# Rows 0 and 2, and rows 1 and 3, as the pairs of a feed-forward unit, with a new written-out order

## The chip, the cores and the metric

One core of a Trainium2 chip runs the kernel. The metric is the device time of one execution in microseconds. TensorE (PE) does the matrix products, VectorE (DVE) and ScalarE (ACT) work elementwise, GpSimd (POOL) does small things, and SyncE (SP) issues most DMAs. Each engine works through its own queue in order and waits on semaphores.

## The reference, cut to what matters

Two layers alternate, each twice, on a sequence of 2048 rows of 512 columns in bf16. `ssm_k` has a filter of 2048 taps for every column, so the product of spectra is a long causal convolution along the sequence.

```python
def _A_ref(q, k, v, shift_k, ssm_k, ssm_D):
    k_shift = causal filter of k with 4 taps (shift_k)
    kv = k_shift * v
    y = irfft(rfft(kv padded to 4096) * rfft(ssm_k padded to 4096))[:2048]
    y = y + kv * ssm_D
    return q * y

def _B_ref(x, w_gate, w_up, w_down):
    g = _silu(x @ w_gate)
    u = x @ w_up
    return (g * u) @ w_down

x = A_q
x = x + _A_ref(_layernorm(x), A_k, A_v, A_shift_k, A_ssm_k, A_ssm_D)
x = x + _B_ref(_layernorm(x), B_w_gate, B_w_up, B_w_down)
x = x + _A_ref(_layernorm(x), A_k, A_v, A_shift_k, A_ssm_k, A_ssm_D)
x = x + _B_ref(_layernorm(x), B_w_gate, B_w_up, B_w_down)
```

(The first line of `_A_ref` and its transforms are abridged here.) The convolved values of both layers A are the same, since they depend on k, v and the filter alone; only q, the normed x, differs.

## The kernel before, in words

The sequence is cut in four chunks of 512 rows (`NB = 4`). A chunk is held as 128 partitions by four "decimated rows": row r holds the positions 4p + r. The convolution is done by blocks: the spectra of a chunk of kv (X) and of the filter (G) are made with cosine and sine matrices on TensorE (`fwd`, `inv`, L310 through the helper `mm`, L457, L796), multiplied on VectorE (`product`, L641 to L666), and turned back. In the inverse of the first chunk (`inverse_half`, L782) VectorE first makes sums and differences of spectral slots (`m`, L790): the decimated rows 0 and 2 come from the sums alone, the rows 1 and 3 from the differences alone. TensorE then makes four products for each row (L796), and ScalarE copies the rows to Y (`evacuate_y`, L716).

A unit of feed-forward work is (layer, chunk c, half h): two of the four decimated rows, which `rows_of(h)` names. There are sixteen units, in the order (0,0,0), (0,0,1), (1,0,0), (1,0,1), and so on by chunk. For every unit `apply_norm` (L869) makes mean and reciprocal deviation: by ScalarE (`ln_stats_act`, L819: jk L827 and L833, nm, ve L837) or by VectorE (`ln_stats`, bnst L808, ve L811), and then the power -0.5 on GpSimd (rstd, L839 or L813). The first layer norm gives n (L858 on ScalarE, with nmr from L851, or L863 on VectorE). `prologue` (L878) multiplies n by Y, adds it to x (L902, L905, L907 in the first two units, L885 and L886 in the others), norms again to z, and transposes z: by TensorE in the first two units (ptz L919, copied to zT by L922 and L924), by a DMA of SP (L892) in the others. `ffn` (L931) multiplies zT by the gate and up weights (pf, L310), ScalarE evacuates (sg L965, ht L969), VectorE multiplies (L972), and TensorE multiplies by the down weights (pd, L985). ScalarE copies pd to dn (L1021) and VectorE adds it (L1024), or x goes through TensorE (L944).

Beside the units runs the conversion of the next chunk: the filter's transform (H, L418 and the butterflies L539, L545, L556), G (L580), the 4-tap filter on TensorE with its copy ks (L513) and product (L514), X and the products.

What sets the order: every operation is first recorded with engine, cost and dependences (`Plan.add`); then `Plan.order` (L186) sorts the recorded operations by `ORDER`, a list with one number for each of the 1569 operations, written out by hand or by a search ahead of time. `Plan.order` also gives tiles to buffers: rings such as `pf` (4 PSUM banks), `pd` (2) and `pc` (2), each free once its last reader stands in the order. `Plan.issue` (L216) emits the operations in that order, so that every engine's queue follows it, and puts warm-up matmuls (L1253) into expected pauses of TensorE in the first 32 us of the plan.

`EVEN` (L45) chooses the rows of a unit:

```python
    def row(h, o):
        return h + HP * o if EVEN else HP * h + o
```

and, in `inverse_half`, the PSUM ring of each row:

```python
        pss = [new(("pd", "pf", "pd", "pf")[r] if EVEN else ("pd", "pd", "pf", "pf")[r], "ps", [P, D], F32) for r in range(R)]
```

Of the kernel before, what the change touches and what calls it, by code (L numbers as in the profile page):

```python
# [44 lines left out]
EVEN = False  # L45
# [192 lines left out]
def kernel(  # L238
# [38 lines left out]
    def row(h, o):  # L277
        return h + HP * o if EVEN else HP * h + o

# [1007 lines left out]
```

## Time and profile before

| what | value |
|---|---|
| median of 3 runs | 347.1 us (346.98, 347.1, 347.27) |
| profiled execution: span from first to last instruction | 345.6 us |
| mean granted TensorE clock | 0.999 |
| busy: PE, DVE, ACT, POOL | 337.1, 283.0, 253.6, 46.5 us |
| first feed-forward matmul (pf, unit (0,0,0)) | 35.58 us |
| last matmul starts up to | 342.2 us |
| DMA | 22.96 MB, mean 66 GB/s |

The profiled execution is one more execution of the same program; the page gives its span, and no time of it in the metric's terms, so the 1.5 us between its span and the median stand for what lies around the span. Times inside the profile are microseconds from the first instruction. Instructions of one engine overlap a little at their ends (a VectorE instruction of 0.69 us is followed by the next after 0.61), so sums of a queue go by the distance from start to start.

### The profile page before, as it was taken

How to read it: one execution, taken by the hardware profiler on the slowest of the kernel's cores; microseconds unless marked ns; L12 is line 12 of the kernel's file. 1: busy time of each engine (PE TensorE's matmuls, PEld its weight loads, DVE VectorE, ACT ScalarE, POOL GpSimd, SP SyncE). 2: the span in 40 equal slices, each digit the busy share in tenths (PEclk: the TensorE clock that was granted, in tenths of full speed). 3: DMA queues.
4: the chain of work that ended last, by engine and by line, in shares of the span. 5: the costliest groups of instructions: out<-in, count | busy, mean ns of one | idle time of the engine just before them, and what ended most of it. 6: DMA issues, size and time to landing. Idle time of an engine off the chain costs nothing.

```text
span 345.6 us, 6557 instructions
## 1 busy us (share of the span) xinstructions
PE 337.1 (98%) x2580; PEld 248.8 (72%) x2612; DVE 283.0 (82%) x481; ACT 253.6 (73%) x503; POOL 46.5 (13%) x46
## 2 busy tenths in 40 slices
PE   8998999999999999999999999999999999999996
PEld 7655867858687767868587867767685868777784
DVE  7897999999999998999999999989998525526120
ACT  6889999989976657878899794569684645446361
POOL 4051111104110101111110000110401000001000
PEclk9999999999999999999999999999999999999999
DMA  7999204030111715010104102130101020101011
GB/s 282 334 306 336 51 14 63 15 93 1 32 31 29 172 40 144 13 34 2 31 3 122 32 0 62 31 93 1 32 0 34 30 32 0 32 0 21 11 47 46
DMA packets 42089, 22.96 MB, mean 66 GB/s; under 512 B 33861, under 2 KB 39882, under 8 KB 42058
## 3 DMA queue, kind: packets, MB, share of 16 engines
q1 hardware_dynamic: 41904, 22.47, 25.3%
q8 instruction: 20, 0.33, 0.4%
q14 instruction: 11, 0.09, 0.1%
q10 hardware_dynamic: 154, 0.07, 0.1%
HBM read 12.33 MB, written 2.10 MB: 42 GB/s over the span
## 4 chain that ended last, share of the span: by engine, by line
PE 92%; ACT 5%; POOL 2%; issue 1%; DVE 0%; ACTq 0%
PE pf L310 55%; PE pd L985 28%; PE ps L310 5%; POOL rstd L839 2%; PE ps L457 1%; PE wm L1253 1%; ACT H L418 1%; ACT n L858 1%; PE pt L476 1%; ACT Yk L716 1%; ACT ks L513 0%; ACT ht L969 0%; PE pt L365 0%; ACT sg L965 0%; ACT hs L486 0%
## 5 line engine op out<-in xcount | busy, mean ns | idle before, releaser
L310 PE MATMUL pf<-zT,wu_sb 128*128 128x256 bf16 x896 | 110.4, 273 | 0.9 <-ACT zT L924 0.7
L310 PE MATMUL pf<-zT,wg_sb 128*128 128x256 bf16 x896 | 110.6, 273 | 0.1
L985 PE MATMUL pd<-wd_sb,ht 128*128 128x512 bf16 (+1 forms) x442 | 100.6, 372 | 1.1
L310 PEld LDWEIGHTS <-wu_sb 128*128 128x128 bf16 x896 | 87.7, 98 | 16.6 <-issue 0.9
L310 PEld LDWEIGHTS <-wg_sb 128*128 128x128 bf16 x896 | 87.7, 98 | 15.4
L969 ACT CAST ht<-pf 128x512 bf16<-128x512 f32 x112 | 64.8, 589 | 30.7 <-PE pf L310 29.2
L965 ACT ACTIVATE sg<-pf 128x512 bf16<-128x512 f32 x112 | 65.6, 601 | 19.1 <-PE pf L310 17.2
L985 PEld LDWEIGHTS <-ht 128*128 128x128 bf16 x462 | 45.0, 98 | 45.2 <-DVE ht L972 0.9
L813 POOL TENSOR_TENSOR rstd<-ve,nhalf 128x2 f32<-128x2 f32 x24 | 27.7, 1153 | 204.5 <-DVE ve L811 204.5
L972 DVE TENSOR_TENSOR ht<-ht,sg 128x1024 bf16<-128x1024 bf16 (+1 forms) x64 | 39.0, 620 | 15.2 <-ACT ht L969 10.2
L1021 ACT CAST dn<-pd 128x512 bf16<-128x512 f32 x28 | 16.1, 590 | 24.1 <-PE pd L985 22.9
L808 DVE BATCH_NORM_STATS2 bnst<-xc 128x6 f32<-128x512 bf16 x48 | 31.7, 686 | 0.7
L1024 DVE TENSOR_TENSOR xc<-xc,dn 128x1024 bf16<-128x1024 bf16 x14 | 9.6, 686 | 18.6 <-ACT dn L1021 18.6
L839 POOL TENSOR_TENSOR rstd<-ve,nhalf 128x2 f32<-128x2 f32 x8 | 15.1, 1892 | 62.4 <-ACT ve L837 62.4
L652 DVE TENSOR_TENSOR t<-X,G 128x2048 bf16<-128x2048 bf16 x18 | 22.0, 1220 | 0.1
L656 DVE TENSOR_TENSOR t<-X,G 128x2048 bf16<-128x2048 bf16 x18 | 21.9, 1217 | 0.0
L418 ACT ACTIVATE X<-ps 128x512 bf16<-128x512 f32 x32 | 18.3, 604 | 1.8 <-PE ps L310 1.4
L885 DVE TENSOR_TENSOR n<-n,Yk 128x1024 bf16<-128x1024 bf16 x15 | 10.3, 689 | 5.8 <-ACT n L858 2.8
L664 DVE TENSOR_TENSOR t<-t,t 128x2048 bf16<-128x2048 bf16 x12 | 14.6, 1220 | 0.2
L666 DVE TENSOR_TENSOR Z<-Z,t 128x2048 bf16<-128x2048 bf16 x12 | 14.6, 1220 | 0.1
L418 ACT ACTIVATE H<-ps 128x512 bf16<-128x512 f32 x24 | 14.1, 609 | 0.7 <-PE ps L310 0.7
L310 PE MATMUL ps<-hs,fwd 128*128 128x512 bf16 x36 | 11.6, 379 | 1.1 <-ACT H L418 1.1
(108 smaller groups left out, 322.5 us busy)
## 6 DMA issues: line engine op xcount, KB each, us to landing
hn<-in_A_ssm_k_dram SPq DMA_DIRECT2D x4, 512.0 KB, 5.8
vt<-in_A_v_dram SPq DMA_DIRECT2D x4, 512.0 KB, 6.1
xc<-in_A_q_dram SPq DMA_DIRECT2D x4, 512.0 KB, 5.1
out_dram<-xc SPq DMA_DIRECT2D x15, 128.0 KB, 1.8
wg_sb<-in_B_w_gate_dram SPq DMA_DIRECT2D x1, 1792.0 KB
wu_sb<-in_B_w_up_dram SPq DMA_DIRECT2D x1, 1792.0 KB, 7.7
wd_sb<-in_B_w_down_dram SPq DMA_DIRECT2D x1, 1280.0 KB, 12.9
kn<-in_A_k_dram SPq DMA_DIRECT2D x1, 512.0 KB, 4.3
```

What stands on the lines that cost most here:

```text
L310: nc.tensor.matmul(o, lhsT=lhsT, rhs=rhs, start=(n == 0), stop=(n == len(terms) - 1))
L418: add("ACT", act(D), lambda: nc.scalar.activation(out=view(), in_=ps.t[:], func=ACT.Copy, scale=scale), r=[ps], w=[(buf, keys)], conv=conv)
L652: dve(n * D, lambda t1=t1, part=part: nc.vector.tensor_mul(out=t1.t[:], in0=x.t[:, sl, 0, :], in1=g.t[:, sl, part, :]), [(x, key(slots, (0 ...
L656: dve(n * D, lambda t2=t2, part=part: nc.vector.tensor_mul(out=t2.t[:], in0=x.t[:, sl, 1, :], in1=g.t[:, sl, 1 - part, :]), [(x, key(slots ...
L808: add("DVE", 0.6, lambda st=st, i=i: nc.vector.bn_stats(out=st.t[:], in_=xs[c].t[:, i, :]), r=[(xs[c], (i,))], w=[st])
L813: add("POOL", pw, lambda: nc.gpsimd.tensor_tensor(out=rstd.t[:], in0=ve.t[:], in1=nhalf.t[:].to_broadcast((P, n)), op=ALU.pow), r=[ve, nha ...
L839: add("POOL", PWA, lambda: nc.gpsimd.tensor_tensor(out=rstd.t[:], in0=ve.t[:], in1=nhalf.t[:].to_broadcast((P, n)), op=ALU.pow), r=[ve, nh ...
L965: add("ACT", act(D), lambda ps=ps, o=o, sg=sg: nc.scalar.activation(out=sg.t[:, o:o + 2, :], in_=ps.t[:], func=ACT.Silu), r=[ps], w=[(sg, ...
L969: add("ACT", act(D), lambda ps=ps, o=o, ht=ht: nc.scalar.copy(out=ht.t[:, o:o + 2, :], in_=ps.t[:]), r=[ps], w=[(ht, (o // 2,))], due=(uni ...
L972: dve(n * W, lambda sg=sg, ht=ht: nc.vector.tensor_mul(out=ht.t[:], in0=ht.t[:], in1=sg.t[:]), [sg], [ht], due=(unit, k / pairs, 0.0, "h"))
L985: nc.tensor.matmul((pds[o] if not cs.start else pds[HP]).t[:, cs], lhsT=ht.t[:, q, o * P:(o + 1) * P], rhs=wt["d"].t[:, ft, cs], start=(ft ...
L1021: add("ACT", act(D), lambda o=o: nc.scalar.copy(out=dn.t[:, o, :], in_=pds[o].t[:]), r=[pds[o]], w=[(dn, (o,))], due=(unit, 1.0, 3.0, "h"))
```

## The change

`EVEN` becomes True: a unit's half 0 has the decimated rows 0 and 2, its half 1 the rows 1 and 3; slices of x, Y and the output rows then have a step of two rows, and in `inverse_half` rows 0 and 2 share the ring `pd`, rows 1 and 3 the ring `pf`. The list `ORDER` is another one in all of its lines; the number of operations is the same.

```diff
-EVEN = False
+EVEN = True
 SUMS = False
...
 ORDER = [
-    0, 3, 66, 2, 4, 5, 16, 31, 1, 27, 22, 23, 28, 29, 8, 6, 7, 9, 10, 32, 12, 11, 13, 14, 15, 34, 33, 35, 54, 55, 56, 24, 36, 25, 38, 26, 43, 39, 40,
...
+    0, 9, 136, 6, 1, 2, 24, 21, 12, 13, 4, 7, 14, 15, 10, 8, 11, 3, 16, 22, 17, 19, 20, 18, 23, 29, 37, 51, 38, 42, 43, 30, 46, 34, 40, 36, 63, 35,
...
```

What the list makes of the queues in the first 40 us: on VectorE the four m (L790) stand as one, then t, Z and three m in a row, all ahead of L902, where before they stood in two pairs; on ScalarE both nmr (L851) stand ahead of n (L858), ve (L837) ahead of the copies of the filter's rows (L486), and zT (L924) ahead of jk (L827); the last of the odd rows' copies to Y (L716) comes behind zT; on TensorE the last product of the odd rows (L796) comes behind the transposes of z (L919). On SP the second part of the down weights is loaded ahead of the first. The warm-up matmuls are 27 instead of 29.

114 rows, old and new, of the table ORDER are left out of this document.

## The prediction

> **What bounds the kernel now.** I read the table of busy times by stretch first, then TensorE's waits, then the timelines of the stretch in which it waits.
>
> ```profile
> core 0: us, PE busy (x) PEld busy (x) DVE busy (x) ACT busy (x) POOL busy (x), PEclk, DMA share, GB/s
> 20.00:30.00 10.00, 8.68 (x64) 4.88 (x64) 8.07 (x17) 8.41 (x18) 5.30 (x1) 1.00 1.04 358
> 30.00:36.00 6.00, 4.85 (x52) 3.44 (x52) 5.64 (x15) 6.00 (x15) 0.80 (x1) 1.00 1.18 288
> 36.00:262.00 226.00, 224.90 (x1690) 167.14 (x1710) 219.31 (x334) 184.53 (x371) 31.36 (x24) 1.00 0.19 43
> ```
>
> From 36 us TensorE is full at the full clock, and its list of waits has nothing after 35.6 us. So the time is the start of the first feed-forward matmul (L310 pf, 35.58) plus a fixed 310 us. But VectorE is 97% busy until 262: a later order can also starve TensorE. The last wait ahead of 35.58 is for ScalarE's copy of zT:
>
> ```profile
> PE ps L310 <- ACT H L418: 1.1, 1, 1.1
> PE pf L310 <- ACT zT L924: 0.7, 1, 0.7
> ```
>
> ScalarE's timeline (start, us, instruction) tells what sets that copy:
>
> ```profile
> 26.08 0.29 ACT L851 ACTIVATE nmr<-nm,rstd 128x1 f32<-128x1 f32 x1 [1.56 <-POOL rstd L839]
> 26.41 0.81 ACT L858 ACTIVATE n<-xc,nmr,rstd 128x512 bf16<-128x512 bf16 x1
> 27.13 0.28 ACT L851 ACTIVATE nmr<-nm,rstd 128x1 f32<-128x1 f32 x1
> 27.32 0.57 ACT L418 ACTIVATE H<-ps 128x512 bf16<-128x512 f32 x1
> 27.79 0.80 ACT L858 ACTIVATE n<-xc,nmr,rstd 128x512 bf16<-128x512 bf16 x1
> ...
> 34.31 0.65 ACT L827 ACTIVATE jk<-xc 128x512 bf16<-128x512 bf16 x1
> ...
> 34.94 0.60 ACT L924 COPY zT<-ptz 128x512 bf16<-128x512 bf16 x1
> ```
>
> It idles 1.56 us for GpSimd's power (rstd), then never again. VectorE meanwhile:
>
> ```profile
> 20.43 0.69 DVE L641 TENSOR_TENSOR t<-X,G 128x1024 bf16<-128x1024 bf16 x1
> 21.03 1.29 DVE L790 TENSOR_TENSOR m<-Z 128x1024 bf16<-128x1024 bf16 x2
> 22.24 1.89 DVE L641 TENSOR_TENSOR t<-X,G 128x1024 bf16<-128x1024 bf16 x3
> 24.05 1.43 DVE L645 TENSOR_TENSOR Z<-t,t 128x512 bf16<-128x512 bf16 x4
> 25.50 1.29 DVE L790 TENSOR_TENSOR m<-Z 128x1024 bf16<-128x1024 bf16 x2
> 28.63 0.69 DVE L902 TENSOR_TENSOR n<-n,ps 128x512 bf16<-128x512 bf16 x1 [1.83 <-ACT n L858]
> ```
>
> It is through with the inverse's sums and differences (m) at 26.80 and waits 1.83 us for ScalarE's n. The differences therefore are not what the first unit waits for; the power is:
>
> ```profile
> 20.75 5.30 POOL L839 TENSOR_TENSOR rstd<-ve,nhalf 128x2 f32<-128x2 f32 x1 [13.99 <-ACT ve L837]
> 38.49 1.01 POOL L839 TENSOR_TENSOR rstd<-ve,nhalf 128x2 f32<-128x2 f32 x1 [5.17 <-ACT ve L837]
> ```
>
> The same instruction takes 0.69 where VectorE idles or runs bn_stats. Everywhere else it ends 0.55 us behind the end of some VectorE instruction: mostly of the one that runs when it starts or just after (38.49: L545 ends at 38.95). Three of the 32 missed that one; two of them (82.28, 246.72, where it took 3.81) ended 0.55 behind the first real pause of VectorE, where an instruction waits for the one before. The third is this first one: the pause is 25.47 to 25.50, ahead of m, and 26.05 is 0.58 behind its beginning.
>
> **The change, part by part.** Queue by queue, the instructions priced by before's rows sum to the same: VectorE 270.2 us, ScalarE 235.8, TensorE 334.2 (0.1 less: two of 29 warm-up matmuls go; the clock stayed 1.00 beside a TensorE wait of 1.1 us, so I price that at nothing). So only order can act. The order differs from the title: VectorE's two differences still stand ahead of L902; behind the first feed-forward matmuls come only the last odd row's evacuation, and ahead of them its last inverse matmul follows the transposes.
>
> 1. *Power, -0.59.* Up to about 22 us TensorE is packed with the same matmuls, so ve is written at 20.65 as before (last X evacuation 19.85, ve 20.34 to 20.65); the power starts at 20.73. One m (0.61 start to start) has moved from ahead of the four Z to behind them. The Z end at 24.87 instead of 25.47; the pause comes then; rstd at 25.46 instead of 26.05.
> 2. *Both nmr ahead of n, -0.17.* Second n at rstd + 1.74 before (26.05 to 27.79). Now nmr 0.19, nmr 0.19, n 0.72, H 0.47: + 1.57, so 27.04.
> 3. *jk (L827) behind zT, -0.63.* Between second n and zT stood twelve evacuations (0.48 to 0.49 each) and jk (34.31 to 34.94). Now twelve without jk (one Yk fewer, one H more). zT at 27.04 + 0.72 + 12 x 0.485 = 33.57, if nothing stalls them.
>
> Sum: -1.39, first pf at 34.2. What else must be there by 33.57: L902 starts at 27.88 behind n; n, n, xc, xc, two bnst, two aggregates, ve (0.60, 0.34, 0.33, 0.34, 0.60, 0.60, 0.13, 0.20, 0.17) end at 31.2; power 0.8 as at 32.52: 32.1; z 32.9; transposes 33.3 and VectorE's half of zT 33.9. The next thing late would be ks of the fourth row: its 16 matmuls wait for the copy of the third (31.74) and end at 32.85, 0.2 before ScalarE comes to it. L905 now waits for a Yk that stands right behind n (28.33), earlier than VectorE gets there (28.49).
>
> 4. *Where behind zT things get later.* jk, X, jk, Yk now stand ahead of unit 0's first evacuations; the fourth pf group waits for Yk (36.4, TensorE gets there at 36.8): hidden, with 0.4 us to spare. The second unit's ve slips from 38.4 to 39.6 us although all else is earlier. SP's queue to the first unit is the same but for wd, whose 1280 KB now go ahead of the 512 KB needed first; all landed by 32.8, needed after 43: nothing.
> 5. *Row pairs.* L886 and L1024 write 128x2x512 with a step instead of 128x1024. Not in the trace; nearest rows: L580 with steps (1.22 for 2048) equals L539 without (1.22), so nothing; the other end is two 128x512 (0.66 against 0.61 start to start), 0.05 x 29 = 1.5 us of VectorE. I take nothing.
> 6. *Hand-overs, +0.2.* VectorE starts its saturated stretch only 0.84 earlier (its zT copy ends 33.92, not 34.76), TensorE 1.39. Adding up both queues to each unit's z: before, the transposed z landed 0.4 to 4.6 us ahead of TensorE. By the new order the units most at risk are the second, eighth and twelfth of the sixteen, with some 0.2, 0.1 and 0.1 left. I charge 0.2 for what they may lose, between 0 and 1.5.
>
> The profiled execution has a span of 345.6; 347.1, the median of the runs, lies 1.5 above it, kept as it is. 345.6 - 1.4 + 0.2 = 344.4, **345.9 us**.
>
> **The rivals.**
>
> *Early power (0.19).* The power catches the end of the VectorE instruction that runs at its start, as most do: 21.14 + 0.55. Then ScalarE reaches nmr by itself at 24.4, L902 waits for the m until 26.8, zT at 32.4: -2.5, with 0.2 charged 344.8. Against it: this very power missed nine such ends before. A rule says so too: the Trainium skill, "SBUF — State Buffer", section "SBUF: two separate sides", has VectorE with two SBUF inputs and GpSimd exclude each other for one whole instruction, the loser waiting for its end. By that rule alone the result is this rival's; the 5.30 and the 3.81 above speak against it, the other rows for it.
>
> *Fixed first power (0.13).* The 5.30 is a cost of the first call, whatever VectorE does; rstd again at 26.1 and only parts 2 and 3 stay: -0.7, 346.6. The Trainium skill, "GPSIMD Engine Reference", section "2.1 Instruction dispatch", gives some 6 us for loading a kernel's code at its first call; by that page this rival is the result. The trace's 3.81 at 246.72, no first call, speaks for the pause.
>
> *Second power stalls: slower (0.19).* Place: rstd of the second unit, power from 39.65. VectorE then runs G (L580, to 41.3), ht, t and waits at L885 at 43.07. If the power misses the first end, that is its first pause: rstd 43.62. ScalarE's queue stands at nmr with ht, X, sg behind it; TensorE wants the buffer that X frees at 44.0 and gets it at 46.6: +2.6, 348.5. It decides from rstd later than about 41.0. For it: three of eight powers of L839 missed. Against: at 38.49 it caught it, with 2.2 us to spare where now there are 0.3.
>
> *The body gives it back (0.14).* VectorE bounds from 36 to 262; the hand-overs lose all that was gained, with 29 stepped instructions dearer at worst: 347.0.
>
> **How the numbers follow.** Forecast 0.35. The range 344.5 to 348.5 holds all five centres, with the low bound of hand-overs; beyond it lie mixtures (a stalled second power on a fixed first) and luck. 0.2% (0.7 us) is about what a measurement tells from no change. Faster (below 346.4): forecast and early power, 0.54. Within: fixed power and given back, 0.27. Slower: 0.19.
>
> **What would show it.** Right: first L839 ends near 25.5, 0.55 to 0.58 behind four Z; L924 near 33.6 with no idle of ScalarE ahead; first pf near 34.2; no TensorE wait beyond it over 0.3. Wrong: L839 of 5.3 again, or ended near 21.7; TensorE waiting for an X or ht near 44; waits for zT's DMA ahead of the eighth or twelfth unit.

## The result and the profile after

The changed kernel takes 344.91 us in the median of 9 runs (344.38 to 345.13), the kernel before, run beside it, 346.69 (344.91 to 347.27, 9 runs). The ratio is 0.9947, 95% interval 0.993 to 0.9964: faster by 0.5%. The profiled execution has a span of 342.92 us against 345.59, 2.67 less.

The table of busy times by stretch (us, then busy time and number of instructions of PE, PEld, DVE, ACT, POOL, TensorE's clock, DMA) and TensorE's waits (total, times, longest), both of the changed kernel:

```profile
20.00:30.00 10.00, 9.20 (x83) 5.72 (x82) 8.88 (x19) 9.02 (x18) 4.75 (x1) 1.00 1.08 357
30.00:36.00 6.00, 5.72 (x54) 4.20 (x54) 5.35 (x13) 6.00 (x16) 0.81 (x1) 1.00 1.19 275
36.00:262.00 226.00, 224.84 (x1681) 166.42 (x1701) 218.19 (x335) 183.24 (x369) 25.73 (x24) 1.00 0.19 42
```

```profile
PE ps L310 <- ACT H L418: 0.4, 1, 0.4
PE ps L310 <- ACT hs L486: 0.3, 1, 0.3
PE ps L310 <- ACT ks L513: 0.2, 1, 0.2
```

Between 20 and 30 us all three engines are busier than before; the body from 36 us on looks the same. The wait for zT is gone from TensorE's list. ScalarE's timeline of the changed kernel (start, length, instruction):

```profile
24.84 0.48 ACT L851 ACTIVATE nmr<-nm,rstd 128x1 f32<-128x1 f32 x2 [0.98 <-POOL rstd L839]
25.23 0.80 ACT L858 ACTIVATE n<-xc,nmr,rstd 128x512 bf16<-128x512 bf16 x1
25.94 0.57 ACT L418 ACTIVATE H<-ps 128x512 bf16<-128x512 f32 x1
26.41 0.80 ACT L858 ACTIVATE n<-xc,nmr,rstd 128x512 bf16<-128x512 bf16 x1
...
32.84 0.69 ACT L924 COPY zT<-ptz 128x512 bf16<-128x512 bf16 x1
```

It idles 0.98 for rstd instead of 1.56, starts both n 1.2 to 1.4 earlier, and reaches zT at 32.84 without jk. VectorE and GpSimd, same kernel:

```profile
22.81 1.42 DVE L645 TENSOR_TENSOR Z<-t,t 128x512 bf16<-128x512 bf16 x4
24.27 1.90 DVE L790 TENSOR_TENSOR m<-Z 128x1024 bf16<-128x1024 bf16 x3
27.25 0.69 DVE L902 TENSOR_TENSOR n<-n,ps 128x512 bf16<-128x512 bf16 x1 [1.09 <-ACT n L858]
```

```profile
20.07 4.75 POOL L839 TENSOR_TENSOR rstd<-ve,nhalf 128x2 f32<-128x2 f32 x1 [13.16 <-ACT ve L837]
38.96 1.19 POOL L839 TENSOR_TENSOR rstd<-ve,nhalf 128x2 f32<-128x2 f32 x1 [7.51 <-ACT ve L837]
```

The four Z end at 24.23, m pauses for them, and the power (L839) ends at 24.81: 0.58 behind the end of the Z, as in the kernel before, but with one m ahead of the pause instead of two; three follow. L902 waits 1.09 for n instead of 1.83. So the step happened as foreseen. Yet the power began at 20.07, not at the forecast 20.73: L457, TensorE's first matmul on v, ran 0.64 earlier than in the profile of before, and the power 0.69. That gain was in no step of the prediction.

To part the two, three distances are used from here on: from the start to that first matmul on v (**L457**), from there to the first feed-forward matmul (**pf**), and from pf to the end.

| kernel | L457 | pf - L457 | last matmul's start - pf | end - last matmul's start | span |
|---|---|---|---|---|---|
| before | 14.46 | 21.12 | 306.32 | 3.69 | 345.59 |
| changed | 13.82 | 19.76 | 306.06 | 3.27 | 342.92 |
| difference | -0.64 | -1.36 | -0.26 | -0.42 | -2.67 |

The forecast was -1.39 in the second column, nothing in the first and the last, and a charge of 0.2 in the third.

### The profile page after: what moved, and what is told of

It reads as the page before. It is cut to its first block, busy times and chain, and to the rows that moved or that the text cites. A ratio compares the mean times of both kernels' runs of the same rounds, so it can differ in the third digit from the quotient of the medians.

```text
span 342.9 us, 6554 instructions
## 1 busy us (share of the span) xinstructions
PE 336.0 (98%) x2578; PEld 247.7 (72%) x2610; DVE 281.6 (82%) x481; ACT 252.0 (73%) x503; POOL 39.4 (11%) x46
## 4 chain that ended last, share of the span: by engine, by line
PE 90%; DVE 4%; ACT 3%; POOL 1%; issue 1%; ACTq 0%
PE pf L310 54%; PE pd L985 28%; PE ps L310 5%; PE ps L457 2%; POOL rstd L839 1%; PE wm L1253 1%; ACT H L418 1%; DVE m L539 1%; ACT Yk L716 0%; ACT n L858 0%; DVE X L545 0%; DVE X L556 0%; DVE ht L972 0%; DVE kTb L373 0%; ACT ks L513 0%
## 5 line engine op out<-in xcount | busy, mean ns | idle before, releaser
L985 PE MATMUL pd<-wd_sb,ht 128*128 128x512 bf16 (+1 forms) x439 | 102.4, 372 | 1.3
L969 ACT CAST ht<-pf 128x512 bf16<-128x512 f32 x112 | 65.6, 596 | 31.6 <-PE pf L310 31.0
L965 ACT ACTIVATE sg<-pf 128x512 bf16<-128x512 f32 x112 | 66.6, 613 | 19.5 <-PE pf L310 17.9
L813 POOL TENSOR_TENSOR rstd<-ve,nhalf 128x2 f32<-128x2 f32 x24 | 23.8, 993 | 198.1 <-DVE ve L811 198.1
L418 ACT ACTIVATE X<-ps 128x512 bf16<-128x512 f32 x32 | 19.0, 618 | 4.7 <-PE ps L310 4.1
L1024 DVE TENSOR_TENSOR xc<-xc,dn 128x1024 bf16<-128x1024 bf16 x14 | 9.6, 684 | 13.4 <-ACT dn L1021 13.4
L839 POOL TENSOR_TENSOR rstd<-ve,nhalf 128x2 f32<-128x2 f32 x8 | 11.7, 1459 | 75.1 <-ACT ve L837 63.4
L885 DVE TENSOR_TENSOR n<-n,Yk 128x1024 bf16<-128x1024 bf16 x15 | 10.3, 689 | 7.8 <-ACT Yk L690 4.5
```

The costliest lines, as they stand in the source:

```text
L418: add("ACT", act(D), lambda: nc.scalar.activation(out=view(), in_=ps.t[:], func=ACT.Copy, scale=scale), r=[ps], w=[(buf, keys)], conv=conv)
L813: add("POOL", pw, lambda: nc.gpsimd.tensor_tensor(out=rstd.t[:], in0=ve.t[:], in1=nhalf.t[:].to_broadcast((P, n)), op=ALU.pow), r=[ve, nha ...
L839: add("POOL", PWA, lambda: nc.gpsimd.tensor_tensor(out=rstd.t[:], in0=ve.t[:], in1=nhalf.t[:].to_broadcast((P, n)), op=ALU.pow), r=[ve, nh ...
L965: add("ACT", act(D), lambda ps=ps, o=o, sg=sg: nc.scalar.activation(out=sg.t[:, o:o + 2, :], in_=ps.t[:], func=ACT.Silu), r=[ps], w=[(sg, ...
L969: add("ACT", act(D), lambda ps=ps, o=o, ht=ht: nc.scalar.copy(out=ht.t[:, o:o + 2, :], in_=ps.t[:]), r=[ps], w=[(ht, (o // 2,))], due=(uni ...
L985: nc.tensor.matmul((pds[o] if not cs.start else pds[HP]).t[:, cs], lhsT=ht.t[:, q, o * P:(o + 1) * P], rhs=wt["d"].t[:, ft, cs], start=(ft ...
```

## The experiments

Theory: the change's own work is the -1.36, by the three moves priced in the prediction; the -0.64 is the moment at which TensorE's clock rises, which differs from one execution to the next. Rivals: the -0.64 comes from the new order of the first operations; the power has a length of its own; the row pairs, not the order, bring the gain. The edits are shown as the order of one engine's instructions, or in words; in the file they are other numbers in `ORDER`. "Ratio" is always to the kernel before, run beside it.

**e1: the order of the first 14 us alone.**

```diff
 ORDER of the kernel before
-its first 110 operations in its own order
+its first 110 operations in the order of the changed kernel
```

> The kernel before, with its first 110 recorded operations (all up to about 14 us) in the order that the change gives them, and all else in its own order. Theory A (the 0.65 us that the first unit gained ahead of the power come from the order of these operations): the first matmul of the spectrum of v (L457) starts near 13.8 instead of 14.46 and the time is 0.65 below the kernel before. Theory B (they come from the moment at which TensorE's matmuls go from one every 107 ns to one every 55 ns, 6.8 us in the profile of before and 4.5 in that of the change, which no order here moves): the order alone is worth under 0.2; L457 follows the moment of the switch in this profile, 14.4 with 6.8, 13.8 with 4.5, and the times of both kernels spread by over 1 us from run to run.

Median 345.51 (345.23 to 347.37), ratio 0.9958 (0.9941 to 0.9975). L457 started at 14.49: no gain there, as theory B says. The time fell all the same, by another way that neither theory had: the power got through at once.

```profile
20.86 0.93 POOL L839 TENSOR_TENSOR rstd<-ve,nhalf 128x2 f32<-128x2 f32 x1 [13.92 <-ACT ve L837]
```

It ended at 21.79, 0.58 behind the end of the t (L641) that ran when it started, with no pause of VectorE behind that t; pf - L457 was 19.52, 1.60 less than before. In the kernel before it had missed the end of the same t, having started 0.32 into it instead of 0.33.

**e2: one m back ahead of the four Z.**

```diff
 VectorE, changed kernel
-Z Z, t, m, t, t, Z Z Z Z, m, m, m
+Z Z, t, m, m, t, t, Z Z Z Z, m, m
```

> The changed kernel with one m (L790) moved back ahead of the last two t and four Z. Pause theory (the first power, L839, gets through at VectorE's first real pause, behind the four Z): that pause and with it rstd come 0.61 later, L839 takes 5.35 us, first feed-forward matmul and time +0.6 (34.2, 345.5). First-call theory (the power has a length of its own): L839 stays at 4.75, rstd at 24.81, time within 0.2 of the changed kernel.

Median 346.15 (345.38 to 349.5), ratio 0.9972 (0.9946 to 0.9997). L839 took 5.35 instead of 4.75 and pf - L457 grew to 20.35, by 0.59. That is the pause theory's number. (L457 was at 15.94 in this profile, ahead of everything that the edit moved. The moved m also changed the planned pauses, which brought three more warm-up matmuls near 27 us; TensorE waits 0.26 for m right behind them, so they held nothing up.)

**e3: jk back ahead of zT.**

```diff
 ScalarE, changed kernel
-ks (L513), zT (L924), jk (L827)
+ks (L513), jk (L827), zT (L924)
```

> The changed kernel with ScalarE's jk (L827) moved back ahead of its copy of zT (L924). If ScalarE's queue alone sets that copy: +0.48 to 0.63, first feed-forward matmul at 34.1 to 34.2, time 345.4 to 345.5. If the transposes ahead of the copy (last at 32.64) or TensorE's own work would have held it anyway, less than 0.3.

Median 345.63 (345.28 to 346.06), ratio 0.995 (0.9934 to 0.9967). pf - L457 is 20.36: +0.60.

**e4: a pause right behind the power's start.**

```diff
 VectorE, changed kernel
-Z Z, t (L641), m (L790), t, t
+Z Z, m (L790), t (L641), t, t
```

> The changed kernel with VectorE's first m (L790) and the t ahead of it exchanged, so that m stands directly behind the Z whose result it reads and VectorE pauses at about 20.5 us, 0.4 behind the power's start. Pause theory: L839 ends 0.55 to 0.58 behind that Z, near 21.1, after some 1.0 us instead of 4.75; ScalarE then reaches nmr by itself at 23.8, 1.0 earlier than the rstd of the changed kernel; if all behind it moves along, the first feed-forward matmul comes at 32.6 and the time is 343.9; if TensorE's inverse or VectorE's m (to 26.2) hold the chain, about half of it. First-call theory: L839 still takes 4.75 and the time stays at 344.9.

Median 343.64 (343.56 to 344.49, 5 runs), ratio 0.9898 (0.9878 to 0.9919): the lowest median of this study. GpSimd and VectorE:

```profile
19.98 0.99 POOL L839 TENSOR_TENSOR rstd<-ve,nhalf 128x2 f32<-128x2 f32 x1 [13.04 <-ACT ve L837]
```

```profile
19.64 0.75 DVE L645 TENSOR_TENSOR Z<-t,t 128x512 bf16<-128x512 bf16 x2
20.43 0.69 DVE L790 TENSOR_TENSOR m<-Z 128x1024 bf16<-128x1024 bf16 x1
```

Z ends at 20.39, m waits 0.03 for it, and the power ends at 20.97, 0.58 behind Z. A first call therefore needs no 4.75 us. pf - L457 is 18.65, 1.11 less than in the changed kernel and 2.47 less than in the kernel before, and no wait of ScalarE for the power is left.

**e5: no warm-up matmuls** (no pause asks for over 1000 of them).

```diff
-                            if n > 0:
+                            if n > 1000:
                                 warm(ring, i, n)
```

> The changed kernel without its 27 warm-up matmuls (wm, L1253). Clock theory (a head start of TensorE's work decides when its matmuls go from one every 107 ns to one every 55, and that moment sets the start of the first spectrum): the transposes and taps up to 8 us or later are all at 107 ns, L457 starts at 15.0 or later instead of 13.82, ve and the power move with it, and the time is 1 to 2 us longer, 346 to 347. If the moment does not matter (TensorE waits there for data anyway), L457 stays within 0.3 of 13.82 and the time within 0.3.

Median 347.07 (346.1 to 348.58), ratio 0.9987 (0.9972 to 1.0002): by the medians the warm-ups are worth as much as the whole change. L457 came at 16.32, 2.50 later than in the first profile of the changed kernel, the power and pf 2.50 and 2.49 later; pf - L457 stayed at 19.75. The moment is passed on in full. How much of the 2.50 the warm-ups made is not shown by one profile: e8, below, has L457 at 15.53 with all its warm-ups. The medians of e5 and e8, taken side by side, differ by 2.16.

**e6: the pause alone, in the kernel before.**

```diff
 VectorE, kernel before
-Z, Z, t (L641), m (L790), m
+Z, t (L641), Z, m (L790), m
```

> The kernel before with one Z and two m of VectorE moved by one place each, so that the first m stands directly behind the Z it reads, at about 21.1 us, 0.35 behind the start of the power (20.75); nothing else is moved. Pause theory: L839 ends near 21.7 after about 1 us instead of 5.30; ScalarE comes to nmr by itself at 24.4, 1.7 earlier than before; the first feed-forward matmul moves by 1.2 to 1.7 (33.9 to 34.4) and the time by as much. If ScalarE's queue, jk and the order of nmr and n are what holds the kernel before (the other parts of the change), less than 0.6.

Median 345.73 (345.46 to 345.99), ratio 0.9947 (0.9931 to 0.9962). L839 took 0.94; pf - L457 fell from 21.12 to 19.57, by 1.55. One instruction moved by one place gains more up to pf than the change with its new list. That the pause is what let the power through is not shown by this run alone, since e1's got through in nearly the same order without one.

**e7: rows paired as before, in the changed order.**

```diff
-EVEN = True
+EVEN = False
 PSUM rings of inverse_half as with EVEN = True
 first unit: L905 behind the first bnst; its Yk copy behind one more H
 two later units: product and copy (L688, L690) of rows 1 and 2 exchanged
 one later unit: those of row 1 put ahead of L885
```

> The changed kernel with rows paired 0 and 1, 2 and 3 as before, in the order of the change, with as few moves as that allows: in the first unit L905 behind the first bnst, its Yk evacuation behind one more H, and two later units' inverse rows exchanged. Theory A (order carries the gain, the pairs none): the first feed-forward matmul 0 to 0.4 later than in the changed kernel, time within 0.4 of it; L886 and L1024 take 0.68 to 0.69 in either. Theory B (the pairs bring it, because row 1 needs the inverse's differences and row 2 does not): L905 waits, the first feed-forward matmul 0.6 to 1.2 later, the time as much.

Median 347.53 (347.04 to 349.73), ratio 1.002 (0.9999 to 1.004). In the first unit pf - L457 was 20.05, +0.29: theory A. But behind pf the last matmul came 2.05 later. The waits between 160 and 265 us, of all engines, show where 1.5 us of it come from:

```profile
DVE n L885 <- ACT Yk L690: 2.5, 1, 2.5
...
PE pd L985 <- DVE ht L972: 1.3, 1, 1.3
```

In a later unit L885 waits for the copy of row 1, whose matmuls read the inverse's differences; row 2 needs the sums alone. So the pairs gain nothing by themselves (L886 takes 689 ns here, 688 in the changed kernel and 691 in that of before; L1024 686, 684 and 686), but the order leans on them. Both theories had half of it.

**e8: the changed kernel again.**

> The changed kernel once more, on the same chip as the three others, to hold them against and for one more look at the moment at which TensorE's matmuls speed up. Clock theory: where that moment differs from 4.5 us, L457, the power's start and the first feed-forward matmul (13.82, 20.07, 33.58) all move by the same amount, and the power's length and all behind it stay. If the order of the first operations alone set them, they are the same to 0.1 whatever the moment is.

Median 344.91 (344.7 to 348.95, 12 runs), ratio 0.9952 (0.9928 to 0.9977). The profile was taken of the run with 348.95. L457 was at 15.53, 1.71 later, pf at 35.27, 1.69 later, pf - L457 19.75. Besides, the rival of the second power came true here; GpSimd and TensorE's waits:

```profile
40.64 4.07 POOL L839 TENSOR_TENSOR rstd<-ve,nhalf 128x2 f32<-128x2 f32 x1 [7.49 <-ACT ve L837]
```

```profile
PE ps L310 <- ACT X L418: 2.4, 1, 2.4
```

The power missed the end of the G (L580) under it, got through at the first pause, ahead of L885, and TensorE, waiting at 47.64 for the buffer that X frees, lost 2.56 (the list has 2.4 of it as a wait). The prediction had priced this at 2.6.

**e9: one output transfer back behind L994.**

```diff
 SP, changed kernel
-L1032 (128 KB), L994, L1001
+L994, L1032 (128 KB), L1001
```

> The changed kernel with one output transfer (L1032, 128 KB, ready long before) put back behind the transfer L994 in SP's queue, where the kernel before has one. Tail theory (the last 64 KB of the output land later when 128 KB go out 2.3 us ahead of them): the last two transfers land 2.1 to 2.3 us after their issue instead of 1.6 to 1.7, the time from the last matmul to the end grows from 3.28 to 3.7 to 3.9, the span behind the first feed-forward matmul from 309.35 to 309.8 to 309.95 and the time by 0.4 to 0.6. If the shorter tail of the changed kernel is chance, all of these stay.

Median 346.44 (344.76 to 349.6), ratio 0.997 (0.9944 to 0.9996), but the end came 3.30 behind the last matmul, as in the changed kernel, and pf - L457 is 19.76. The tail theory falls. Five runs lie near 345.0, five near 346.5 and two above, and the one profile, of a run at 345.13, does not tell why.

**e10: five more warm-up matmuls, with e4's pause.**

```diff
-                        n = int((start - max(t, 0.3) - 0.3) / 0.106)
+                        n = int((start - max(t, 0.3) - 0.3) / 0.106) + (5 if 3.0 < start < 8.0 and t > 2.0 else 0)
```

> The kernel of the moved m (first m directly behind its Z) with 5 more warm-up matmuls (L1253) ahead of the first transposes, so that TensorE does not idle between 4.4 us and the arrival of the kernel's first rows (4.5 to 4.9). Clock theory (the switch comes at the end of a stretch of 3.41 us in which TensorE was hardly idle, and a gap of 0.4 us there costs another 3.41): the switch comes no later than 7.9 us; where the rows arrive early the 5 cost up to 0.5 at L457 (13.74 to 14.2) and up to that in time, 343.6 to 344.1, and no run is above 346. If gaps play no part, the runs spread as those of the changed kernel do, up to 347 and more.

Median 345.25 (344.52 to 348.36), ratio 0.9952 (0.9931 to 0.9973). L457 14.04 with the clock's rise at 4.46, pf - L457 18.67, as in e4. One run at 348.36 is against the expectation, and behind pf TensorE lost 0.92 in one wait at 227.5 which e4 does not have. The trace has it as a wait for the DMA of a transposed z (L892): that transfer landed 3.99 us after its issue, where the same one in e4 took 2.48, and a transfer of instructions ran beside it, from 225.34 to 226.38, which in e4 began at 226.75, when the z had landed. What five more warm-ups do to the spread stays open.

**e11: the second nmr back behind the first n.**

```diff
 ScalarE, changed kernel
-nmr (L851), nmr, n (L858), H, n
+nmr (L851), n (L858), nmr, H, n
```

> The changed kernel with ScalarE's second nmr (L851) back behind the first n (L858), as in the kernel before. If the working of that step holds: the second n ends its wait 0.10 to 0.17 later behind the power (starts at rstd + 1.70 to 1.77 instead of 1.60), and the first feed-forward matmul as much later behind L457 (19.86 to 19.93 instead of 19.76). If other work hides it: 19.76 stays.

344.92 in its one run. The second n starts at rstd + 1.74 instead of + 1.60; pf - L457 is 19.89: +0.13.

**e12: a pause for the second power.**

```diff
 VectorE, changed kernel
-G, G (L580), ht, t (L652), n (L885), xc, t (L656)
+G, G (L580), t (L656), ht, t (L652), n (L885), xc
```

> The changed kernel with VectorE's t (L656) moved up directly behind the second G (L580) it reads, so that VectorE pauses there, some 1.8 us behind the start of the second unit's power (L839); ht (L972) goes one place, 1.2 us, back. Theory A (the runs of the changed kernel at 346.5 and more are those in which that power misses the end of the first G and TensorE then waits 2.4 us for an X, as in the one trace with 348.95): no run has a power of over 2.4 us there, the stall shrinks from 2.56 to at most 0.9, and the runs above 346 are gone or are at most 1.5 above the lowest; ht costs up to 0.2 in each. Theory B (they come from the late start of the first spectrum, L457 at 15 to 16 us): the share of runs above 346 stays as it was, about a third of 24 on these two days.

Median 345.19 (344.96 to 345.48, 5 runs), ratio 0.9954 (0.9941 to 0.9968). The power caught the first G in the profiled execution anyway (1.19); the later ht cost 0.13 behind pf, at 43 us. No run is above 346, but neither is any of the nine runs of the changed kernel beside its first profile. Inconclusive.

## Why the prediction was right, and where it was not

**The three moves** were right in kind and size. Undone one at a time:

| step | forecast | measured, pf - L457 |
|---|---|---|
| 1, power behind one m fewer | -0.59 | -0.59 (e2) |
| 2, both nmr ahead of n | -0.17 | -0.13 (e11) |
| 3, jk behind zT | -0.63 | -0.60 (e3) |
| sum | -1.39 | -1.32; together -1.36 |

**The premise of step 1** ("Up to about 22 us TensorE is packed with the same matmuls, so ve is written at 20.65 as before") is what failed. TensorE's first transposes, kernel before, then changed kernel (start, length of the group):

```profile
4.50 1.86 PE L476 MATMUL pt<-ident,hn 128*128 128x128 bf16 x16
6.16 1.21 PE L365 MATMUL pt<-ident,kn 128*128 128x128 bf16 x12
```

```profile
4.48 1.05 PE L476 MATMUL pt<-ident,hn 128*128 128x128 bf16 x16
5.63 0.84 PE L365 MATMUL pt<-ident,kn 128*128 128x128 bf16 x12
```

They start together, and TensorE's instructions up to them are the same; but sixteen take 1.86 us in the one and 1.05 in the other, a matmul every 107 ns against every 55. By the trace's record of the granted clock it rises at 6.94 us in the profile of before and at 4.29 in that of the changed kernel. Over all profiles:

| clock rises at | 4.29 | 4.78 | 4.83 | 5.65 | 6.26 | 6.31 | 6.46 | 6.73 | 6.94 | 8.72 | 9.59 | 10.12 |
|---|---|---|---|---|---|---|---|---|---|---|---|---|
| L457 | 13.82 | 13.89 | 13.74 | 13.84 | 14.14 | 14.15 | 14.22 | 14.49 | 14.46 | 15.53 | 15.94 | 16.32 |
| kernel | changed | e11 | e4 | e6 | e12 | e7 | e9 | e1 | before | e8 | e2 | e5 |

(e10, with five more matmuls ahead, has 4.46 and 14.04; for e3 no record of the rise is left.) Both orders of the first operations lie on one line (before and e6 have the old one), so the order there is worth some 0.1 at most, and the -0.64 is chance between two executions: e8, the changed kernel once more, has 8.72 and 15.53. The Trainium skill, "TensorE: Matmul & The Clock Gate", section "What's actually happening", has the clock raised after a busy window of 3413 ns that runs freely and does not begin with the kernel. e8's 8.72 against the 4.29 of the same program agrees, and the recorded stretches at full clock are 98, 99 or 100 times 3.413 us long. That the rises spread over more than one such window would need windows that did not count as busy; e2 and e8 had TensorE idle for 0.4 us ahead of the transposes, and e10, which fills that gap, does not settle it. The same page of the Trainium skill, section "What you observe", gives 107 and 56 ns for such matmuls, the traces 107 and 55.

Medians of these kernels carry that chance too, so a term of 0.1 to 0.6 us was read here from the distances in a profile and not from the medians.

**The fixed 310 us behind pf** were 310.01 in the kernel before and 309.33 in the changed one, in three kernels of the old order 310.01 to 310.26 and, where no other wait was added, 309.33 to 309.36 in those of the new. Of this 0.26 are two TensorE waits for ht at 246.6 and 262.4 us (0.16 and 0.09), in all three of the old order and in none of the new. The other 0.4 lie behind the last matmul. DMA of the last microseconds, kernel before, then changed (queue, packets, MB, share; transfer, KB, us to landing):

```profile
q14 instruction: 1, 0.01, 1.2%
...
out_dram<-xc SPq DMA_DIRECT2D x1, 64.0 KB, 2.1
```

```profile
out_dram<-xc SPq DMA_DIRECT2D x1, 64.0 KB, 1.6
```

In the three kernels of the old order a transfer of instructions starts within 0.4 us of the last output's data, and the end is 3.69 to 3.94 behind the last matmul's start; in the eleven of the new order there is none, and it is 3.27 to 3.30. That the one causes the other was not tried by itself; e9 excludes the output transfer ahead of it. The transposes of z (L892) show the same coincidence more often: over all profiles 324 of them have a traced landing, 306 within 2.57 us of their issue and 18 after 2.72 to 4.43, and beside each of these 18 ran a transfer of instructions of 0.96 to 1.33 us.

**Hand-overs, charged 0.2 (0 to 1.5)**: nothing was lost in the profile of the changed kernel. With the two waits gone the term had the other sign, -0.26.

**Row pairs, nothing**: right as a cost. That the order needs them (e7) was not in the prediction.

**The sum.** From the profile of before, 1.36 + 0.26 + 0.42 = 2.0 us is the change's own, where 1.2 was forecast; 0.64 more was luck of the two profiles. The forecast span of 344.4 thus came out 1.5 too long: 0.6 by the clock's rise, 0.5 by the hand-overs (-0.26 for +0.2), 0.4 by the tail. What lies around the span is 1.78 (344.70 for the profiled 342.92), not 1.5, which took back 0.3, and the profiled run lies 0.2 below its median. So the forecast of 345.9 was 1.0 above the median of 344.91: right in kind, and 0.6 of what it missed was luck.

**The rivals.** *Fixed first power* is refuted: L839 took 0.93 in e1, 0.94 in e6, 0.99 in e4. The 6 us that the Trainium skill, "GPSIMD Engine Reference", section "2.1 Instruction dispatch", has for the first call of freshly loaded code are not seen in this kernel. *Early power* did not happen in the changed kernel, but does with one instruction exchanged (e4), at -2.47 up to pf where -2.5 was forecast. *Second power stalls* happened in one of ten profiles with that order of the second unit (e8), at the forecast price. With the late L457 it makes up that run's 348.95; what made the other runs above 346 was not profiled, and the median, 344.91 as in the first nine runs, does not show it. *The body gives it back*: it did not.

**Open.** What decides whether the power takes the end of the instruction under it or must await a pause. In nine profiles with the changed kernel's order at that place the first power started 2 to 8 ns behind a Z and missed every end up to the pause, so it is no coin toss there; but the second power started 569 ns behind G in e5 and in e8 and caught its end in one and missed it in the other. The rule of the Trainium skill, "SBUF — State Buffer", section "SBUF: two separate sides" (one instruction, then through), which the prediction weighed, agrees with most powers and not with these. Open too is whether the kernel before gets its power through at once by chance: two of its nine runs, 344.91 and 344.99, lie 1.7 below its median, near the 1.60 that e1 gained in this way, but neither was profiled.

## What to carry to other kernels

Where a GpSimd instruction on the critical path (here a power of 128x2 numbers) runs beside a VectorE that never pauses, put an instruction that reads its predecessor's result just behind the start of the GpSimd instruction: 0.03 us of pause bought 1.1 us in e4, against nine profiles without it whose power missed, and went with 1.55 in e6. Before comparing two profiles, look at the spacing of the first matmuls; if it differs, count from the first instruction behind the clock's rise, or the luck of two executions is read as an effect of the code. A new order leans on what it was found with, as this one on the row pairs: parts of such a change can't be priced apart by their own cost alone.

## What the runs showed of the hardware

- The first power of 128x2 numbers took 0.93 to 0.99 us where it got through at once and 4.74 to 5.35 where it waited for VectorE's first pause. In every profile it ended 0.58 us behind the end of a VectorE instruction; without a pause behind that instruction in e1 alone.
- The table of busy times by stretch shows TensorE's clock as 1.00 in both kernels between 4 and 7 us, where the spacing of the matmuls, 107 ns, shows half speed in the kernel before; the spacing is the surer sign.
- Without the 27 warm-up matmuls L457 came 2.50 us later than in the first profile of the changed kernel and 0.80 later than in e8's, and all of it reached the first feed-forward matmul.
- No transpose of z landed later than 2.57 us after its issue without a transfer of instructions beside it; with one of 0.96 to 1.33 us, 18 landed after 2.72 to 4.43, and one of these, in e10, cost TensorE 0.92 us. No run took such a transfer away.
